# A fourth sum on TensorE in a rational feed-forward behind sketched attention

## The chip, the cores and the metric

The kernel runs on one core of a Trainium2 chip. The metric is the time of one execution on the device in microseconds (us); lower is better. Engines: PE is TensorE (matmuls; PEld its weight loads), DVE is VectorE, ACT is ScalarE, POOL is GpSimd, SP is SyncE, which issues most DMAs. L12 is line 12 of the kernel.

## The reference

Inputs are q, k, v of shape (4 batches, 4 heads, 1088 tokens, 32) in fp32, two sketches S1, S2 of 8 x 32, and the weights of a feed-forward layer: w_in 128 x 2048, w_out 2048 x 128, a (4 numbers) and b (2 numbers). Cut to what matters:

```python
phi(x) = outer(S1 @ x, S2 @ x)                 # 64 features per token and head
kv, z  = sum over tokens of phi(k) * v, phi(k)
x      = (phi(q) @ kv) / (phi(q) @ z + 1e-6)   # heads side by side: 4352 x 128
h      = x @ w_in
g      = (a0 + a1*h + a2*h**2 + a3*h**3) / (1 + |b0|*|h| + |b1|*h**2 + 1e-6)
out    = g @ w_out
```

## The kernel before

**Attention.** For each batch the keys are transposed on DVE in 32 x 32 blocks (`kt`, L255), sketched by TensorE (`ks`, L263), copied by ACT (`kc`, L270), multiplied into features on DVE (`kf`, L275) and summed with v by TensorE (`kp`, L304); ACT keeps the result (`kk`). The queries go in blocks of 256 to 384 tokens, 13 in all: transposition (`qt`, L327), sketches (`qs`), copies (`qc`), features (`qf`), product with kv on TensorE (`qp`, L368), denominator (`qd`, L377 or L380), its inverse (`qi`, L384), quotient on DVE (`qx`, L389), back transposition on TensorE (`qb`, L395), and ACT keeps xT (`qk`, L402). From the fourth block on the sketches take a way through DRAM to be spread over the partitions (L419 to L436).

**Feed-forward.** h and g are kept with the 2048 hidden columns on the partitions, 128 at a time, and tokens along the free axis. The work is cut into 17 units of 4096 elements per partition: unit 0 holds 256 tokens with all 16 column blocks, units 1 to 14 hold 512 tokens with 8 blocks each (two units per group of tokens; the even ones take blocks 8 to 15), units 15 and 16 again 256 tokens with 16 blocks. A unit has two half units of 2048; half unit n belongs to unit n // 2. Steps of a unit, with the letters of the order:

- `h` (L459): TensorE computes a quarter of h in fp32 into one of two PSUM buffers of 1024; `e` (L465): ACT copies it to hh in bf16.
- `u`, `w`, `y` (L488, L494, L499): DVE computes |h|, then |b1||h| + |b0|, then times |h|, for the denominator.
- `ln`, `ex` (L550, L554): ACT computes r = exp(-ln(denominator)), a half unit at a time.
- `p`: the linear factor a3·h + a2, on ACT (`pa`, L545) or DVE (`pd`, L540), as the list P_ON_ACT says.
- `s` (L558): s = h·r. `m` (L562): g = h·s. `x` (L573): g = g·p, thus h·h·r·(a3·h + a2). All on DVE.
- `G` (L592): TensorE adds r with w_out·a0, s with w_out·a1 and g with w_out, three sums per half unit, into one PSUM bank per group of tokens.
- In the half units of HORNER, g = h·p, plus a1 (`v`, L568), times s; only r and g are summed.
- `st` (L601, L609): DVE transposes the bank and four or more DMAs store it.

The scaled copies of w_out are made once, by halves (`wo`, L625 to L629).

**The order.** Nothing is scheduled by the machine: each engine works through its instructions in the order of the list ORDER, which is written out, with the step's name and its unit, block or batch. An engine that waits holds up all that stands behind it. r, s and g have four buffers of a half unit each, p has two, hh three of a unit. Loads are steps too (`lk`, `lq`, `lv`, `lw`, `lx` for k, q, v, w_out and w_in); all of them go into SyncE's queue.

Of the kernel before, what the change touches and what calls it, by code (L numbers as in the profile page):

```python
# [20 lines left out]
ORDER = """
tn:4 tn:0 lw:1 lq:0 kt0:0 lw:0 kt1:0 lx:1 kt2:0 lx:0 ks1:0 kt3:0 ks0:0 lk:1 qt:0 ks2:0 kc0:0 kc1:0 kf0:0 kf1:0 qs:0
kc2:0 qt:1 kf2:0 qc:0 kp0:0 ba:0 kp1:0 qf:0 kp2:0 wo:3 qs:1 kk:0 lv:1 qt:2 qp:0 qc:1 wo:1 qf:1 qs:2 qd:0 qi:0 qc:2
qp:1 qx:0 qf:2 wo:0 qb:0 qp:2 qd:1 qi:1 qk:0 qx:1 qt:3 h3:0 qd:2 qi:2 lq:1 qx:2 wo:4 wo:2 h2:0 e3:0 kt1:1 h0:0 kt0:1
e2:0 pa1:0 u1:0 lk:2 qs:3 w1:0 qb:2 h1:0 y1:0 qc:3 qk:2 e0:0 qt:5 qb:1 ks0:1 qt:4 e1:0 qs:4 qk:1 u0:0 ln1:0 h1:1 qt:6
w0:0 y0:0 kc0:1 ex1:0 h2:1 kf0:1 ks1:1 e1:1 s1:0 e2:1 h0:1 m1:0 kc1:1 ln0:0 kf1:1 h3:1 lq:2 e0:1 x1:0 e3:1 h1:2 kt0:2
ex0:0 u1:1 h2:2 qf:3 w1:1 qc:4 e1:2 qp:3 e2:2 s0:0 pa0:0 h3:2 y1:1 h0:2 qd:3 wo:5 e3:2 qi:3 m0:0 G0:0 e0:2 qx:3 G1:0
ln0:1 kt1:2 x0:0 qb:3 ks0:2 u1:2 qk:3 G2:0 ex0:1 lk:3 pd0:1 G3:0 w1:2 G4:0 pa1:1 kp1:1 y1:2 kc0:2 ln1:1 G5:0 qf:4 lv:2
qs:5 kf0:2 kk:1 ex1:1 qp:4 s0:1 ks1:2 qd:4 qc:5 qi:4 ln0:2 qt:7 G0:1 qx:4 m0:1 qb:4 G1:1 qk:4 s1:1 ex0:2 h3:3 x0:1
kc1:2 h2:3 m1:1 e3:3 kf1:2 h0:3 e2:3 kt1:3 ln1:2 s0:2 h1:3 st:0 m0:2 e0:3 qs:7 x1:1 e1:3 h2:4 ex1:2 u1:3 h3:4 pd1:2  # L30
pa0:2 w1:3 kp1:2 s1:2 e2:4 x0:2 e3:4 h0:4 lv:3 qf:5 pa0:3 y1:3 qp:5 qc:7 e0:4 h1:4 m1:2 qd:5 ln0:3 qi:5 qt:9 G2:1 qx:5
e1:4 x1:2 qb:5 G3:1 qk:5 u1:4 ex0:3 G4:1 m0:3 G5:1 pa1:3 G0:2 w1:4 h0:5 kt0:3 ln1:3 m1:3 h2:5 y1:4 kk:2 ex1:3 ks0:3
G1:2 e0:5 s1:3 G2:2 ln0:4 G3:2 h1:5 v0:3 ex0:4 qf:7 x0:3 G4:2 e2:5 qs:6 s0:4 qc:6 h3:5 e1:5 pd0:4 ln1:4 m0:4 h1:6 v1:3
e3:5 x0:4 pa1:4 h0:6 u1:5 qt:8 G5:2 e1:6 w1:5 ex1:4 h3:6 st:2 y1:5 e0:6 qp:7 e3:6 s1:4 G0:3 pa0:5 lq:3 G2:3 x1:3 qs:8
m1:4 h2:6 ln0:5 m0:5 G3:3 e2:6 x1:4 G5:3 ex0:5 qf:6 G0:4 u1:6 G1:4 qc:8 qd:7 ln1:5 qi:7 qp:6 w1:6 G2:4 qx:7 qd:6 pa0:6
qi:6 v0:5 qb:7 G3:4 qx:6 y1:6 qb:6 qk:7 G4:4 qk:6 ex1:5 h3:7 m0:6 pa1:5 G5:4 s1:5 h1:7 e3:7 st:4 h2:7 m1:5 e1:7 ln0:6
x0:5 h0:7 qt:10 x1:5 e2:7 G0:5 e0:7 qf:8 ks1:3 kc0:3 ex0:6 u1:7 qs:9 h1:8 v0:6 qc:9 w1:7 ln1:6 h3:8 s0:6 e1:8 pd1:6
qp:8 ex1:6 y1:7 h0:8 e3:8 s1:6 kc1:3 ln0:7 h2:8 x0:6 e0:8 m1:6 G2:5 qd:8 ex0:7 G3:5 qi:8 kf0:3 G4:5 kf1:3 G5:5 e2:8
qs:10 ln1:7 u1:8 kp1:3 qx:8 w1:8 ex1:7 qb:8 G0:6 qf:9 qk:8 y1:8 qc:10 h3:9 pa0:7 s0:7 h0:9 e3:9 s1:7 ln0:8 h2:9 qt:12
m0:7 e0:9 G0:7 x1:6 e2:9 h1:10 ex0:8 x0:7 qt:11 h1:9 u1:9 pa0:8 m1:7 G2:6 pd1:7 e1:9 G3:6 s0:8 e1:10 G4:6 u0:9 ln1:8  # L40
h3:10 w1:9 m0:8 qp:9 ex1:8 x1:7 h2:10 x0:8 qd:9 kk:3 e3:10 qi:9 w0:9 pa0:9 h0:10 qf:10 y0:9 qp:10 e2:10 y1:9 e0:10
G5:6 qx:9 qd:10 ln0:9 qi:10 qb:9 s1:8 G1:7 qx:10 G2:7 qk:9 u1:10 ex0:9 G3:7 m1:8 qb:10 G4:7 qk:10 s0:9 ln1:9 G5:7
qs:11 pd1:8 h1:11 w1:10 qc:11 ex1:9 x1:8 h0:11 e1:11 m0:9 pa1:9 h3:11 y1:10 e0:11 G0:8 s1:9 e3:11 h2:11 ln0:10 x0:9
h0:12 m1:9 e2:11 pd0:10 ex0:10 h1:12 u1:11 x1:9 e0:12 G1:8 w1:11 e1:12 G2:8 ln1:10 G3:8 s0:10 G4:8 y1:11 G5:8 ex1:10
qs:12 G0:9 m0:10 G1:9 ln0:11 h3:12 s1:10 ex0:11 x0:10 h2:12 qf:11 pa1:10 m1:10 G2:9 s0:11 G3:9 e3:12 G4:9 x1:10 qc:12
ln1:11 qp:11 pd0:11 m0:11 G5:9 qd:11 e2:12 G0:10 qi:11 x0:11 ex1:11 G1:10 u1:12 G2:10 pa1:11 qx:11 G3:10 w1:12 qb:11
G4:10 qk:11 s1:11 pa0:12 h1:13 y1:12 h3:13 e1:13 m1:11 ln0:12 h2:13 st:6 x1:11 ex0:12 G5:10 qf:12 G0:11 st:8 e3:13
qp:12 s0:12 e2:13 st:10 h0:13 ln1:12 m0:12 u1:13 h2:14 e0:13 x0:12 ex1:12 u0:13 h3:14 w1:13 w0:13 e2:14 y1:13 e3:14
h1:14 pa1:12 y0:13 h0:14 s1:12 qd:12 e1:14 qi:12 m1:12 G1:11 e0:14 qx:12 G2:11 ln1:13 u1:14 qb:12 G3:11 pd0:13 G4:11
ex1:13 w1:14 G5:11 x1:12 G0:12 qk:12 ln0:13 h0:15 s1:13 pd1:13 ex0:13 G1:12 y1:14 G2:12 e0:15 h2:15 s0:13 ln0:14 m1:13  # L50
h3:15 e2:15 m0:13 ex0:14 h1:15 x1:13 x0:13 e3:15 G3:12 s0:14 e1:15 h2:16 ln1:14 u1:15 G4:12 m0:14 ex1:14 G5:12 w1:15
G0:13 h3:16 pa0:14 st:12 y1:15 G1:13 e2:16 G2:13 s1:14 e3:16 h1:16 ln0:15 u2:16 u3:16 w2:16 w3:16 h0:16 x0:14 ex0:15
y2:16 G3:13 pd0:15 e0:16 G4:13 s0:15 e1:16 G5:13 y3:16 pa1:14 G0:15 u0:16 m0:15 G1:15 ln1:15 G0:14 m1:14 G1:14 w0:16
G2:14 ex1:15 x0:15 G3:14 y0:16 G2:15 v1:14 G3:15 ln0:16 s1:15 x1:14 ex0:16 pd1:15 G5:14 m1:15 G0:16 ln2:16 s0:16 G4:15
pa0:16 x1:15 G1:16 ex2:16 m0:16 G5:15 ln3:16 s2:16 x0:16 ex3:16 m2:16 G2:16 pa2:16 st:15 s3:16 G3:16 pa3:16 G4:16
st:14 x2:16 m3:16 G5:16 G6:16 x3:16 G7:16 G8:16 st:16
""".split()
# [12 lines left out]
def kernel(  # L70
    ctx: ExitStack,
# [466 lines left out]
    def d_p(i, h, hh):
        if not on_act(i, first(h)):
            nc.vector.tensor_scalar(out=part_of(i, "p", h), in0=hh, scalar1=a3, scalar2=a2, op0=AX.mult, op1=AX.add)  # L540

    @skip(WIDE_P, on_act)
    def a_p(i, h, hh):
        if on_act(i, first(h)):
            nc.scalar.activation(out=part_of(i, "p", h), in_=hh, func=ACT.Identity, scale=a3_reg, bias=a2)  # L545

# [21 lines left out]
            nc.vector.tensor_scalar(out=g, in0=g, scalar1=a1, scalar2=None, op0=AX.add)  # L568

    @skip(WIDE_X, horner)  # L570
    def d_g(i, h, hh):
        g = part_of(i, "g", h)
        nc.vector.tensor_mul(out=g, in0=g, in1=part_of(i, "s" if horner(i, first(h)) else "p", h))  # L573
# [9 lines left out]

    def gather(i, part):
        t0, tl, f0, per = units[i]
        if t0 not in outs:
            outs[t0] = bank()
            summed[t0] = [0, sum(len(z) for j in range(NU) if units[j][0] == t0 for z in terms(j))]
        for x, y, key in terms(i)[part]:
            done = summed[t0]  # L590
# [1 line left out]
            nc.tensor.matmul(outs[t0][:, :tl], lhsT=w_sb[y][:, f0 + x, :], rhs=part_of(i, key, h)[:, c:c + tl],  # L592
                             start=done[0] == 0, stop=done[0] == done[1] - 1)
# [25 lines left out]
    QC = Queries(0, q0, cuts[2], cuts[3])  # L619

    def w_part(x):
        y, f = x // 2, x % 2 * (nf // 2)
        o, t = w_sb[y][:, f:f + nf // 2], w_out_sb_f[:, f:f + nf // 2]
        if y == 2:
            (nc.scalar.copy if W_ENG[x] else nc.vector.tensor_copy)(out=o, in_=t)  # L625
        elif W_ENG[x]:
            nc.scalar.activation(out=o, in_=t, func=ACT.Copy, scale=a_sb[:, y:y + 1])
        else:
            nc.vector.tensor_scalar(out=o, in0=t, scalar1=a_sb[:, y:y + 1], scalar2=None, op0=AX.mult)  # L629
# [93 lines left out]
```

## Time and profile before

| | |
|---|---|
| median of 3 runs | 270.98 us (270.41 to 271.04) |
| the profiled execution's own time | 271.85 us |
| its span, from the first to the last instruction | 270.1 us |
| busy: PE, DVE, ACT | 252.6, 255.7, 246.9 us |
| granted TensorE clock, mean | 0.99 |

How to read it: the profile shows one execution. A group row gives engine, operation, out<-in, partitions x elements and type, count, then busy us and mean ns of one, then the idle time ahead of it with what ended it. A timeline row gives start, duration, engine, line. Matmul ends are modelled, since matmuls are pipelined. A row of the table of stretches gives for each stretch the busy time of PE, PEld, DVE, ACT and POOL, the granted clock, and the share and GB/s of the DMA.

### The profile page before, as it was taken

How to read it: one execution, taken by the hardware profiler on the slowest of the kernel's cores; microseconds unless marked ns; L12 is line 12 of the kernel's file. 1: busy time of each engine (PE TensorE's matmuls, PEld its weight loads, DVE VectorE, ACT ScalarE, POOL GpSimd, SP SyncE). 2: the span in 40 equal slices, each digit the busy share in tenths (PEclk: the TensorE clock that was granted, in tenths of full speed). 3: DMA queues.
4: the chain of work that ended last, by engine and by line, in shares of the span. 5: the costliest groups of instructions: out<-in, count | busy, mean ns of one | idle time of the engine just before them, and what ended most of it. 6: DMA issues, size and time to landing. Idle time of an engine off the chain costs nothing.

```text
span 270.1 us, 4166 instructions
## 1 busy us (share of the span) xinstructions
PE 252.6 (94%) x1598; PEld 136.0 (50%) x1613; DVE 255.7 (95%) x278; ACT 246.9 (91%) x224; POOL 2.9 (1%) x24
## 2 busy tenths in 40 slices
...
DMA packets 30531, 19.57 MB, mean 72 GB/s; under 512 B 20400, under 2 KB 26672, under 8 KB 30512
## 3 DMA queue, kind: packets, MB, share of 16 engines
q1 hardware_dynamic: 28864, 18.92, 26.8%
...
## 4 chain that ended last, share of the span: by engine, by line
DVE 43%; PE 28%; ACT 12%; issue 8%; DMA 6%; SPq 1%; DVEq 0%; ACTq 0%
PE att_ps L592 14%; PE h_ps L459 12%; DVE w L499 7%; DVE s L558 6%; DVE g L562 6%; DVE g L573 5%; DVE w L494 4%; ACT ln L550 4%; DMA k_sb<-in_k_dram 4%; DVE u L488 4%; ACT hh L465 3%; DVE k_p L275 3%; ACT r L554 3%; DMA q_sb<-in_q_dram 2%; DVE q_pT L436 2%
## 5 line engine op out<-in xcount | busy, mean ns | idle before, releaser
L459 PE MATMUL h_ps<-xT,w_in_sb 128*128 128x512 f32 (+1 forms) x320 | 126.2, 538 | 3.7 <-ACT hh L465 2.8
L459 PEld LDWEIGHTS h_ps<-xT,w_in_sb 128*128 128x128 f32 x320 | 58.2, 190 | 56.7 <-issue 36.9
L465 ACT CAST hh<-h_ps 128x1024 bf16<-128x1024 f32 x68 | 67.7, 1026 | 4.5 <-PE h_ps L459 4.3
L592 PEld LDWEIGHTS <-w_out 128*128 128x128 bf16 x460 | 45.0, 99 | 47.2 <-issue 15.0
L550 ACT ACTIVATE ln<-w 128x2048 f32<-128x2048 bf16 (+1 forms) x35 | 66.1, 1888 | 0.8 <-DVE w L499 0.6
L554 ACT ACTIVATE r<-ln 128x2048 bf16<-128x2048 f32 (+1 forms) x35 | 65.8, 1879 | 0.6
L545 ACT ACTIVATE p<-hh,a_sb 128x2048 bf16<-128x2048 bf16 (+1 forms) x23 | 44.6, 1942 | 0.2 <-DVE g L573 0.2
L558 DVE TENSOR_TENSOR s<-hh,r 128x2048 bf16<-128x2048 bf16 (+2 forms) x33 | 40.9, 1242 | 0.0
L499 DVE TENSOR_TENSOR w<-w,u 128x4096 bf16<-128x4096 bf16 (+2 forms) x22 | 39.3, 1794 | 0.1
L592 PE MATMUL att_ps<-g,w_out 128*128 128x512 bf16 (+1 forms) x155 | 34.8, 350 | 4.6 <-DVE g L573 3.9
L592 PE MATMUL att_ps<-r,w_out 128*128 128x512 bf16 (+1 forms) x155 | 35.1, 354 | 1.1 <-ACT sk_sb L419 0.7
L562 DVE TENSOR_TENSOR g<-hh,s 128x2048 bf16<-128x2048 bf16 (+1 forms) x30 | 35.1, 1172 | 0.0
L573 DVE TENSOR_TENSOR g<-g,p 128x2048 bf16<-128x2048 bf16 (+1 forms) x30 | 35.0, 1173 | 0.1
L592 PE MATMUL att_ps<-s,w_out 128*128 128x512 bf16 (+1 forms) x135 | 29.2, 342 | 0.2
L494 DVE TENSOR_SCALAR w<-u,b_abs 128x4096 bf16<-128x4096 bf16 (+2 forms) x22 | 23.8, 1089 | 0.0
L488 DVE TENSOR_SCALAR u<-hh 128x4096 uint16<-128x4096 uint16 (+2 forms) x22 | 21.2, 968 | 0.0
L368 PEld LDWEIGHTS att_ps<-kvz,q_pT 128*64 128x64 f32 x288 | 9.6, 137 | 7.3 <-DVE q_pT L436 2.0
L368 PE MATMUL att_ps<-kvz,q_pT 128*64 128x66 f32 x288 | 11.5, 226 | 0.1
L255 DVE STREAM_TRANSPOSE kT<-k_sb 128x224 f32<-128x224 f32 (+4 forms) x10 | 5.9, 614 | 4.6 <-DMA k_sb<-in_k_dram 4.6
L304 PEld LDWEIGHTS att_ps<-v_sb,k_p 128*64 128x64 f32 (+1 forms) x288 | 8.8, 138 | 2.4 <-DVE qT L327 1.1
L304 PE MATMUL att_ps<-v_sb,k_p 128*64 128x64 f32 (+1 forms) x288 | 9.3, 223 | 0.7 <-DMA v_sb<-in_v_dram 0.7
L540 DVE TENSOR_SCALAR p<-hh,a_sb 128x2048 bf16<-128x2048 bf16 x12 | 9.7, 804 | 0.0
...
## 6 DMA issues: line engine op xcount, KB each, us to landing
...
```

The source lines that it names most:

```text
L459: nc.tensor.matmul(t[:, x * tl:(x + 1) * tl], lhsT=w_in_sb[:, f * 128:(f + 1) * 128], rhs=xT[:, x_at(t0):x_at(t0) + tl], start=True, stop= ...
L465: nc.scalar.copy(out=live[i]["hh"][:, part * PW:(part + 1) * PW], in_=live[i]["h", part])
L488: nc.vector.tensor_scalar(out=t[:, c].bitcast(U16), in0=live[i]["hh"][:, c].bitcast(U16), scalar1=0x7FFF, scalar2=None, op0=AX.bitwise_and)
L494: nc.vector.tensor_scalar(out=t[:, c], in0=live[i]["u"][:, c], scalar1=ab1, scalar2=ab0, op0=AX.mult, op1=AX.add)
L499: nc.vector.tensor_mul(out=t[:, c], in0=t[:, c], in1=live[i]["u"][:, c])
L545: nc.scalar.activation(out=part_of(i, "p", h), in_=hh, func=ACT.Identity, scale=a3_reg, bias=a2)
L550: nc.scalar.activation(out=t, in_=live[i]["w"][:, span(h)], func=ACT.Ln, bias=1.0 + 1e-6)
L554: nc.scalar.activation(out=part_of(i, "r", h), in_=live[i]["ln"], func=ACT.Exp, scale=-1.0)
L558: nc.vector.tensor_mul(out=part_of(i, "s", h), in0=hh, in1=part_of(i, "r", h))
L562: nc.vector.tensor_mul(out=part_of(i, "g", h), in0=hh, in1=part_of(i, "p" if horner(i, first(h)) else "s", h))
L573: nc.vector.tensor_mul(out=g, in0=g, in1=part_of(i, "s" if horner(i, first(h)) else "p", h))
L592: nc.tensor.matmul(outs[t0][:, :tl], lhsT=w_sb[y][:, f0 + x, :], rhs=part_of(i, key, h)[:, c:c + tl], start=done[0] == 0, stop=done[0] == ...
```

## The change

In 11 of the 34 half units (FOUR) the linear factor p is not formed. There `x` writes h·g = h·h·h·r into a p buffer, `G`'s third part sums g = h·h·r with w_out·a2, and a new step `F` sums h·h·h·r with w_out·a3. Two more scaled copies of w_out are made for this, for column blocks 8 to 15 alone, since all 11 half units lie there. HORNER shrinks from five half units to three (7 and 29 leave it; 29 is in FOUR). P_ON_ACT changes: p is left on DVE in half units 1, 2, 8, 15 and 27. The lists of wide steps M, X and P are emptied; a wide step is formed only where both halves of the unit agree. ORDER is new from end to end. The diff, with ORDER cut to its first lines:

```diff
-tn:4 tn:0 lw:1 lq:0 kt0:0 lw:0 kt1:0 lx:1 kt2:0 lx:0 ks1:0 kt3:0 ks0:0 lk:1 qt:0 ks2:0 kc0:0 kc1:0 kf0:0 kf1:0 qs:0
-kc2:0 qt:1 kf2:0 qc:0 kp0:0 ba:0 kp1:0 qf:0 kp2:0 wo:3 qs:1 kk:0 lv:1 qt:2 qp:0 qc:1 wo:1 qf:1 qs:2 qd:0 qi:0 qc:2
-qp:1 qx:0 qf:2 wo:0 qb:0 qp:2 qd:1 qi:1 qk:0 qx:1 qt:3 h3:0 qd:2 qi:2 lq:1 qx:2 wo:4 wo:2 h2:0 e3:0 kt1:1 h0:0 kt0:1
...
+tn:4 ba:0 kt3:0 tn:0 kt1:0 ks1:0 lq:0 kt0:0 kt2:0 ks0:0 ks2:0 kc1:0 kf1:0 qt:0 kc0:0 lk:1 kf0:0 qs:0 kc2:0 kp0:0 qc:0
+kp1:0 kf2:0 kp2:0 qt:1 qt:2 qs:1 qf:0 kk:0 lx:1 qp:0 kt0:1 qc:1 qd:0 lw:1 qi:0 qx:0 kt1:1 qf:1 qs:2 lw:0 qb:0 qt:3
+ks0:1 qk:0 kc0:1 h3:0 kf0:1 wo:7 wo:3 lx:0 qc:2 h2:0 qs:3 qf:2 wo:4 wo:6 e3:0 lk:2 qp:2 e2:0 wo:2 lq:1 pd1:0 qd:2 wo:1
+u1:0 qp:1 ks1:1 qd:1 qc:3 qi:2 qi:1 kc1:1 qx:2 h0:0 wo:5 qx:1 qb:1 qb:2 e0:0 h1:0 qk:1 w1:0 qk:2 kf1:1 y1:0 e1:0 ln1:0
...
-W_ENG = (1, 1, 0, 0, 0, 1)
-P_ON_ACT = (1, 1, 0, 1, 1, 0, 1, 1, 0, 1, 1, 1, 1, 0, 1, 0, 1, 0, 1, 1, 0, 1, 0, 1, 1, 1, 0, 0, 1, 1, 0, 0, 1, 1)
+W_ENG = (1, 1, 0, 0, 0, 1, 1, 0)
+P_ON_ACT = (1, 0, 0, 1, 1, 0, 1, 1, 0, 1, 1, 1, 1, 1, 1, 0, 1, 0, 1, 1, 0, 1, 1, 1, 1, 1, 1, 0, 1, 1, 1, 0, 1, 1)
-WIDE_M = (5,)
-WIDE_X = (5, 14)
-WIDE_P = (2,)
-HORNER = (6, 7, 10, 12, 29)
+WIDE_M = ()
+WIDE_X = ()
+WIDE_P = ()
+HORNER = (6, 10, 12)
+FOUR = (5, 9, 13, 17, 20, 21, 24, 25, 28, 29, 31)
...
+    w_more = [big.tile([128, nf // 2, d_model], BF, name=f"w_more_{i}") for i in range(2)]
...
     def d_g(i, h, hh):
         g = part_of(i, "g", h)
+        if four(i, first(h)):
+            nc.vector.tensor_mul(out=part_of(i, "p", h), in0=hh, in1=g)
+            return
         nc.vector.tensor_mul(out=g, in0=g, in1=part_of(i, "s" if horner(i, first(h)) else "p", h))
...
-        return [[(x, y, key) for x in range(*c)] if y != 1 or not horner(i, n) else []
-                for n, c in enumerate(cuts) for y, key in enumerate(("r", "s", "g"))]
+        return [[(x, y, key) for x in range(*c)] if (y != 1 or not horner(i, n)) and (y != 3 or four(i, n)) else []
+                for n, c in enumerate(cuts) for y, key in enumerate(("r", "s", "g", "p"))]
 
     def gather(i, part):
+        sums(i, part // 3 * 4 + part % 3)
+
+    def gather_four(i, part):
+        sums(i, part * 4 + 3)
...
-            nc.tensor.matmul(outs[t0][:, :tl], lhsT=w_sb[y][:, f0 + x, :], rhs=part_of(i, key, h)[:, c:c + tl],
+            w = w_sb[y][:, f0 + x, :] if y < 2 or not four(i, part // 4) else w_more[y - 2][:, f0 + x - nf // 2, :]
+            nc.tensor.matmul(outs[t0][:, :tl], lhsT=w, rhs=part_of(i, key, h)[:, c:c + tl],
                              start=done[0] == 0, stop=done[0] == done[1] - 1)
```

More of the change, by code (lines that the diff above doesn't have):

```diff
@@ L21 @@
 ORDER = """
-tn:4 tn:0 lw:1 lq:0 kt0:0 lw:0 kt1:0 lx:1 kt2:0 lx:0 ks1:0 kt3:0 ks0:0 lk:1 qt:0 ks2:0 kc0:0 kc1:0 kf0:0 kf1:0 qs:0
-kc2:0 qt:1 kf2:0 qc:0 kp0:0 ba:0 kp1:0 qf:0 kp2:0 wo:3 qs:1 kk:0 lv:1 qt:2 qp:0 qc:1 wo:1 qf:1 qs:2 qd:0 qi:0 qc:2
-qp:1 qx:0 qf:2 wo:0 qb:0 qp:2 qd:1 qi:1 qk:0 qx:1 qt:3 h3:0 qd:2 qi:2 lq:1 qx:2 wo:4 wo:2 h2:0 e3:0 kt1:1 h0:0 kt0:1
-e2:0 pa1:0 u1:0 lk:2 qs:3 w1:0 qb:2 h1:0 y1:0 qc:3 qk:2 e0:0 qt:5 qb:1 ks0:1 qt:4 e1:0 qs:4 qk:1 u0:0 ln1:0 h1:1 qt:6
-w0:0 y0:0 kc0:1 ex1:0 h2:1 kf0:1 ks1:1 e1:1 s1:0 e2:1 h0:1 m1:0 kc1:1 ln0:0 kf1:1 h3:1 lq:2 e0:1 x1:0 e3:1 h1:2 kt0:2
@@ L27 @@
[L27 to L56, printed above, removed]
+tn:4 ba:0 kt3:0 tn:0 kt1:0 ks1:0 lq:0 kt0:0 kt2:0 ks0:0 ks2:0 kc1:0 kf1:0 qt:0 kc0:0 lk:1 kf0:0 qs:0 kc2:0 kp0:0 qc:0
@@ new lines @@
+kp1:0 kf2:0 kp2:0 qt:1 qt:2 qs:1 qf:0 kk:0 lx:1 qp:0 kt0:1 qc:1 qd:0 lw:1 qi:0 qx:0 kt1:1 qf:1 qs:2 lw:0 qb:0 qt:3
+ks0:1 qk:0 kc0:1 h3:0 kf0:1 wo:7 wo:3 lx:0 qc:2 h2:0 qs:3 qf:2 wo:4 wo:6 e3:0 lk:2 qp:2 e2:0 wo:2 lq:1 pd1:0 qd:2 wo:1
+u1:0 qp:1 ks1:1 qd:1 qc:3 qi:2 qi:1 kc1:1 qx:2 h0:0 wo:5 qx:1 qb:1 qb:2 e0:0 h1:0 qk:1 w1:0 qk:2 kf1:1 y1:0 e1:0 ln1:0
+qt:4 h2:1 qt:5 e2:1 kt0:2 h1:1 u0:0 qs:4 kt1:2 ks0:2 ex1:0 w0:0 qt:6 ks1:2 y0:0 s1:0 kc0:2 qf:3 lv:1 e1:1 qc:4 h0:1
+m1:0 qs:5 kf0:2 x1:0 ln0:0 e0:1 h3:1 qp:3 h3:2 e3:1 u1:1 ex0:0 e3:2 s0:0 h2:2 qd:3 wo:0 pa0:0 qi:3 w1:1 kc1:2 e2:2
@@ new lines @@
+qx:3 kp1:1 y1:1 h1:2 m0:0 kk:1 qf:4 lq:2 qc:5 qb:3 h0:2 ln0:1 qk:3 G4:0 qp:4 G3:0 x0:0 qt:7 e1:2 qd:4 G5:0 qi:4 pd0:1
+qx:4 e0:2 u1:2 qs:7 qt:8 lk:3 qb:4 w1:2 ex0:1 s0:1 kf1:2 G1:0 qk:4 G2:0 h0:3 y1:2 h2:3 pa1:1 kt1:3 ln1:1 G0:0 qf:5
+kt0:3 qc:7 e0:3 e2:3 h1:3 m0:1 h3:3 ex1:1 e1:3 qp:5 s1:1 ln0:2 qd:5 e3:3 ex0:2 h2:4 G0:1 qi:5 m1:1 h3:4 e2:4 qs:6 u1:3
+h1:4 e3:4 G4:1 h0:4 x0:1 qx:5 s0:2 w1:3 qf:7 lv:2 x1:1 qb:5 qc:6 kp1:2 ln1:2 ex1:2 y1:3 e1:4 qt:9 qk:5 e0:4 s1:2 kk:2
+u1:4 st:0 m0:2 h1:5 G2:1 qs:8 ln0:3 qp:7 qf:6 ex0:3 m1:2 G3:1 pa0:2 ks0:3 G1:1 w1:4 qc:8 ln1:3 G0:2 x0:2 qd:7 h3:5
@@ new lines @@
+x1:2 e1:5 y1:4 qp:6 pa0:3 qd:6 e3:5 kc0:3 ex1:3 G3:2 F1:2 h0:5 qi:6 qi:7 h2:5 qx:6 e0:5 e2:5 qx:7 ln0:4 ex0:4 qb:7
+G0:3 m0:3 s1:3 G1:2 pd0:4 pa1:3 G5:1 h0:6 u1:5 kf0:3 m1:3 G4:2 h3:6 w1:5 e0:6 v0:3 lq:3 qk:7 y1:5 ln1:4 G2:2 e3:6 x1:3
+ex1:4 G3:3 s0:4 qb:6 h2:6 qk:6 qf:8 e2:6 G5:2 qs:9 h1:6 G1:4 G0:4 h0:7 m0:4 x0:3 ln0:5 G2:3 qc:9 ex0:5 s1:4 e1:6 ks1:3
+x0:4 m1:4 st:2 lv:3 pa0:5 qp:8 G4:3 u1:6 kc1:3 m0:5 G4:4 x1:4 ln1:5 w1:6 G2:4 h3:7 e0:7 ex1:5 e3:7 qt:11 h1:7 G5:3
+h2:7 qd:8 pa0:6 y1:6 e1:7 qt:10 e2:7 F1:4 h0:8 kf1:3 G5:4 qs:10 s1:5 qi:8 qf:9 ln0:6 pa1:5 qx:8 G3:4 u1:7 m1:5 ex0:6
@@ new lines @@
+h2:8 G4:5 G0:5 qc:10 ln1:6 e0:8 ex1:6 e2:8 kp1:3 m0:6 w1:7 v0:6 G3:5 h3:8 y1:7 st:4 s1:6 qb:8 qp:9 x1:5 kk:3 ln0:7
+m1:6 qk:8 v0:5 h1:8 e3:8 G5:5 x1:6 ex0:7 e1:8 qd:9 pa0:7 G0:6 qf:10 s0:6 h0:9 e0:9 h1:9 ln1:7 u1:8 qi:9 w1:8 x0:6 x0:5
+qp:10 h2:9 G4:6 ex1:7 y1:8 s0:7 F1:6 qd:10 s1:7 e1:9 qs:11 G2:6 u0:9 G5:6 G2:5 qi:10 G3:6 m0:7 h3:9 e2:9 pd1:7 ln0:8
+ex0:8 m1:7 qc:11 h0:10 qx:9 e3:9 ln1:8 s0:8 h3:10 qx:10 qb:9 G3:7 e0:10 e3:10 w0:9 h2:10 qb:10 ex1:8 G0:7 qt:12 y0:9
+G1:7 m0:8 u1:9 s1:8 qk:9 e2:10 x0:7 w1:9 ln0:9 G4:8 qf:11 qs:12 m1:8 qk:10 h1:10 ex0:9 x1:7 e1:10 y1:9 G4:7 h0:11
@@ new lines @@
+qc:12 pa0:8 h2:11 x1:8 ln1:9 qp:11 F1:8 st:6 e0:11 u1:10 G0:8 G5:7 h1:11 qd:11 x0:8 ex1:9 G2:8 s0:9 qi:11 w1:10 e2:11
+h3:11 qx:11 pa1:9 s1:9 e1:11 G1:8 G2:7 y1:10 qb:11 pa0:9 e3:11 qf:12 ln0:10 m0:9 h2:12 G1:9 u1:11 qp:12 h3:12 ex0:10
+m1:9 w1:11 e2:12 ln1:10 G3:8 e3:12 s0:10 x1:9 ex1:10 h0:12 qk:11 G1:10 h1:12 y1:11 x0:9 e0:12 G5:8 G0:9 ln0:11 h3:13
+s1:10 m0:10 e1:12 G4:9 m1:10 x0:10 u1:12 G0:10 G3:9 x1:10 F0:10 G5:9 qd:12 ex0:11 ln1:11 e3:13 ex1:11 h2:13 pa0:11
+G2:10 G3:11 w1:12 s0:11 y1:12 F1:10 qi:12 s1:11 st:8 e2:13 u1:13 qx:12 m1:11 w1:13 h0:13 ln0:12 e0:13 ex0:12 G2:9
@@ new lines @@
+pa1:11 m0:11 h1:13 qb:12 e1:13 h0:14 ln1:12 s0:12 x0:11 G5:10 G3:10 e0:14 h3:14 e3:14 G1:11 m0:12 u0:13 y1:13 x1:11
+h1:14 G4:11 w0:13 x0:12 ex1:12 e1:14 y0:13 qk:12 G4:10 s1:12 ln1:13 h2:14 e2:14 h1:15 st:10 m1:12 u1:14 ex1:13 x1:12
+w1:14 e1:15 s1:13 h0:15 G0:11 h3:15 G5:11 F1:12 ln0:13 y1:14 m1:13 e0:15 e3:15 ex0:13 pd1:13 G3:12 G0:12 h2:15 G1:12
+ln0:14 G2:11 e2:15 ex0:14 s0:13 F0:12 x1:13 pa0:13 u1:15 ln1:14 ex1:14 h1:16 m0:13 w1:15 G4:12 G2:12 G4:13 e1:16 s0:14
+y1:15 h0:16 G0:13 G5:12 m0:14 x0:13 e0:16 h3:16 G2:14 ln0:15 s1:14 G3:13 x0:14 u0:16 G3:14 m1:14 ex0:15 h2:16 w0:16
```

19 lines of the change are left out of this document (14 added, 5 removed).

## The prediction

> **What bounds the kernel now.** I read the busy shares first, then six stretches of the span, the waits of VectorE, and the timeline at both ends.
>
> ```profile
> span 270.1 us, 4166 instructions
> PE 252.6 (94%) x1598; PEld 136.0 (50%) x1613; DVE 255.7 (95%) x278; ACT 246.9 (91%) x224; POOL 2.9 (1%) x24
> ```
> ```profile
> 0.00:17.50 17.50, 14.76 (x195) 9.39 (x195) 10.78 (x27) 6.79 (x17) 2.94 (x24) 1.00 0.80 241
> 17.50:26.80 9.30, 8.77 (x56) 7.11 (x56) 6.45 (x12) 6.47 (x9) 0.00 (x0) 1.00 0.80 203
> 26.80:140.00 113.20, 109.02 (x779) 55.77 (x786) 112.72 (x112) 111.49 (x104) 0.00 (x0) 1.00 0.30 82
> 140.00:250.00 110.00, 107.71 (x484) 54.84 (x491) 109.83 (x111) 109.28 (x88) 0.00 (x0) 1.00 0.15 33
> 250.00:266.80 16.80, 12.34 (x87) 8.90 (x86) 15.94 (x20) 12.89 (x10) 0.00 (x0) 0.90 0.13 19
> 266.80:270.10 3.30, 0.00 (x0) 0.00 (x0) 0.00 (x0) 0.00 (x0) 0.00 (x0) 0.72 0.43 65
> ```
> Columns of the second fence: stretch, length, busy PE, weight loads, DVE, ACT, POOL, granted clock, DMA. Between 26.8 and 250 DVE works 222.55 of 223.2 us: it never waits. ACT idles 2.4 us there. So every microsecond taken from DVE counts at once, as long as ACT (2.4 us of room) and TensorE can follow. Of DVE's 14.4 idle us, 9.6 lie before 26.8, one wait among them:
>
> ```profile
> DVE kT L255 <- DMA k_sb<-in_k_dram: 2.7, 1, 2.7
> ```
> ```profile
> 22.20 1.37 DVE L255 STREAM_TRANSPOSE kT<-k_sb 128x224 f32<-128x224 f32 x2 [2.68 <-DMA k_sb<-in_k_dram]
> 26.77 1.95 ACT L550 ACTIVATE ln<-w 128x2048 f32<-128x2048 bf16 x1
> ```
> ```profile
> 11.41 10.77 DMA k_sb<-in_k_dram
> ```
> The second batch's keys, issued at 11.41, land at 22.2 while DVE stands still (the third fence is from the chain of waits); the first logarithm starts at 26.77.
>
> How much room has TensorE? Its 94% says hardly any. Its rows overlap, though, so I go by the distance from one start to the next:
>
> ```profile
> 245.35 1.04 PE L592 MATMUL att_ps<-r,w_out 128*128 128x256 bf16 x8
> 246.22 1.04 PE L592 MATMUL att_ps<-s,w_out 128*128 128x256 bf16 x8
> 247.10 1.03 PE L592 MATMUL att_ps<-r,w_out 128*128 128x512 bf16 x4
> ```
> ```profile
> 235.85 1.89 PE L459 MATMUL h_ps<-xT,w_in_sb 128*128 128x256 f32 x8
> 237.58 1.03 PE L592 MATMUL att_ps<-s,w_out 128*128 128x512 bf16 x4
> ```
> A w_out sum of one half unit lasts 1.04 but takes 0.87 us (246.22 to 247.10 and the one before). A hidden block of eight 256 wide matmuls lasts 1.89 and takes 1.73. The Trainium skill, "Perfetto Trace Analysis", Identifying the Most-Contended Engine, has the same reservation: matmul busy time is a bad measure of headroom because matmuls are pipelined, while for VectorE and ScalarE occupancy is fair. By busy time the sum would be 252.6 + 11.2 added (below) + 5.0 at the two ends = 268.8 without any idle left, so next to no gain could be had; by starts there is room, as follows.
>
> ```profile
> L459 PE MATMUL h_ps<-xT,w_in_sb 128*128 128x512 f32 x224 | 103.9, 604 | 3.0 <-ACT hh L465 2.6 <-ACT xT L402 0.2
> L459 PE MATMUL h_ps<-xT,w_in_sb 128*128 128x256 f32 x96 | 22.4, 383 | 0.7 <-DMA w_in_sb<-in_moe_w_in_dram 0.5 <-ACT hh L465 0.2
> L368 PE MATMUL att_ps<-kvz,q_pT 128*64 128x66 f32 x240 | 9.2, 226 | 0.1
> ```
> ```profile
> 17.58 5.42 PE L459 MATMUL h_ps<-xT,w_in_sb 128*128 128x256 f32 x24 [0.48 <-DMA w_in_sb<-in_moe_w_in_dram]
> ```
> ```profile
> 266.28 0.45 DVE L601 STREAM_TRANSPOSE out_sb<-att_ps 128x256 f32<-128x256 f32 x1 [0.69 <-PE att_ps L592]
> ```
> From the first hidden matmul (17.58) to the last sum (266.3) are 248.7 us. The work in it: 224 records at 0.43 and 96 at 0.216 are 117; the 316 sums of 512 at 0.217 and 144 of 256 at 0.109 (counted in the instruction order, since records are missing) are 84; the attention matmuls, taken at some nine tenths of their rows' 33 busy us (the L368 row is the largest of them), are an estimated 29.5. That makes 230, and leaves 18.5 us free, not the 6 or so that busy time shows. After the last sum come 3.8 us: transposition and store.
>
> **The change, part by part.** The instruction orders of both kernels give the counts.
>
> ```profile
> L545 ACT ACTIVATE p<-hh,a_sb 128x2048 bf16<-128x2048 bf16 x21 | 42.4, 2019 | 0.2 <-DVE g L573 0.2
> L540 DVE TENSOR_SCALAR p<-hh,a_sb 128x2048 bf16<-128x2048 bf16 x12 | 9.7, 804 | 0.0
> L568 DVE TENSOR_SCALAR g<-g,a_sb 128x2048 bf16<-128x2048 bf16 x5 | 3.7, 732 | 0.0
> L573 DVE TENSOR_TENSOR g<-g,p 128x2048 bf16<-128x2048 bf16 x28 | 33.6, 1209 | 0.0
> L627 ACT ACTIVATE w_out<-w_out_sb_f,a_sb 128x1024 bf16<-128x1024 f32 x2 | 2.3, 1157 | 0.0
> L629 DVE TENSOR_SCALAR w_out<-w_out_sb_f,a_sb 128x1024 bf16<-128x1024 f32 x2 | 1.5, 750 | 0.6 <-DMA w_out_sb_f<-in_moe_w_out_dram 0.6
> ```
> ```profile
> 48.12 0.73 DVE p L540
> 65.69 1.14 DVE g L573
> 94.29 0.66 DVE g L568
> ```
> The second fence is from the chain of waits, where an instruction counts until the next starts: successive DVE instructions overlap by about 0.07 us, and I take 0.07 off each.
> - *Linear factor p.* In 11 half units it is gone. With the new division between engines 5 remain on DVE (12 before) and 18 half units' worth on ACT (22 before). DVE: 7 x 0.73 = -5.1. ACT: 4 x 1.95 = -7.8.
> - *Horner* in 3 instead of 5: the added a1 goes twice, 2 x 0.66 = -1.3 on DVE. Their products stay the same in number.
> - *The product h·h·h·r* takes the place of g·p: same form as L573, 1.21 each, no difference.
> - *Two more scaled halves of w_out*: +0.7 on DVE, +1.1 on ACT.
> - *TensorE:* 11 further sums at 0.87 = 9.5, and the two half units that are no longer Horner sum s as well: 2 x 0.87 = 1.7. Together +11.2.
> - *The wide lists* emptied: costs nothing. By their conditions only the two wide s were ever formed, and these stay.
>
> So DVE -5.7, ACT -6.7, TensorE +11.2.
>
> ```profile
> 10.00:20.00 10.00, 9.34 (x149) 7.74 (x150) 7.92 (x18) 4.82 (x14) 0.00 (x0) 1.00 1.07 327
> ```
> ```profile
> 14.87 0.15 DVE L377 TENSOR_SCALAR den<-att_ps 128x8 f32<-128x8 f32 x1
> 21.31 1.01 ACT L465 CAST hh<-h_ps 128x1024 bf16<-128x1024 f32 x1 [0.71 <-PE h_ps L459]
> ```
> ```profile
> 30.40 1.14 DVE k_p L275
> 33.93 1.40 DVE k_p L275
> ```
> *The start.* SyncE now issues the rest of q, then the second batch's keys, half of w_in, both halves of w_out, the other half of w_in; before, w_out and w_in stood ahead of the keys. DVE has the key transposes (L255) between the first block's q products and its denominator, so that a late landing holds back the first x and the first hidden matmul. Landing: the stretch from 10 to 20 us moved 327 GB/s; ahead are 0.30 MB of q and 0.56 MB of k, 2.6 us from 10, and w_in's half in the kernel before landed some 1.9 us after the same sum: I estimate 14.5 us, against bounds of 12.6 (no lag) and 22.2 (as now). The denominator, at 14.87 now, would come at about 15.5, the first hidden matmul at 17.3: unchanged within 0.5. In return the keys' products (1.14 and 1.40), a w_out half (0.68) and a p (0.74) stand ahead of the first logarithm, and 1.6 us of transposes and absolute values behind it: 2.4 us of DVE work fill what was the wait. Next late is the second hidden evacuation (ending at 22.3 now, about 22.0 then); from it DVE has 5.7 us up to the first logarithm: 27.8 instead of 26.8. Start: -2.4 + 1.0 = -1.4 by DVE.
>
> *New waits.* A p buffer that holds h·h·h·r is released by TensorE's sum and no longer by DVE; behind it waits the next unit's p on ACT, and behind that the logarithms. In the order each such sum stands ahead of that p, and it costs nothing while TensorE is less than a unit (223 us over 17 units, some 13 us) behind; if the cover is gone, an ACT row of 1.95 us is late each time, at most 11 times. I take 0 to 4 us of this into the range.
>
> **The sum.** DVE's bound: 270.1 - 5.7 - 1.4 = 263.0, if it goes on without waits. TensorE's: first hidden matmul 17.3, work 230 + 11.2 + 0.6 (moved behind it at the start) = 242, then 3.8: 263.1, if it never waits. ACT, with 6.7 taken off and 2.4 idle between 26.8 and 250 already, ends no later. So three engines end together, none with room for the others, where before DVE was alone at the limit. Some waiting must come back: bounds 0 and 18.5 (all of today's). I take 4, since TensorE today restarts with a loss of about 0.1 us after each wait (25 waits on hh), and since the tail's last products must be waited for anyway. Span 263 + 4 = 267, that is -3.1. The profiled execution took 271.85 with a span of 270.1, the median of the runs is 270.98; so 270.98 - 3.1 = 267.9, say **268.0**.
>
> The tail today shows what a pause of TensorE costs:
>
> ```profile
> 254.51 0.51 PE L592 MATMUL att_ps<-g,w_out 128*128 128x512 bf16 x1 [2.05 <-DVE g L573]
> ```
> ```profile
> 256.00:258.00 2.00, 2.00 (x10) 1.32 (x9) 2.00 (x3) 2.00 (x2) 0.00 (x0) 0.50 0.00 0
> ```
> After 2.05 us without work the clock is granted at half for a while; a sum then takes twice 0.87. Today it is hidden behind DVE. "TensorE: Matmul & The Clock Gate", The HAM clock gate, in the Trainium skill puts the threshold at one idle window of about 3.4 us; here a pause of 2.05 within busy surroundings was enough, so the measurement decides. It speaks neither for nor against the sum: with a fuller TensorE such pauses grow rarer, and one of them costs some 1.7 us.
>
> **Rivals.**
> 1. *TensorE becomes the bound and keeps its waits* (slower). Its queue is in order: behind a hidden block that waits for one of two h buffers stand the sums, and with seven of the eleven four-fold half units in units 10 to 15 there is no free time there to catch up in. For it: 18.5 us of waiting today, and the hidden matmuls with their weight loads stood 25 times for hh:
>
> ```profile
>   ACT hh L465: 15.8, 25
> ```
> Against it: today's waits are largely those of an engine that is early. Price: 263.1 plus the waits left. From 7 us on nothing is gained; at 10, span 273, time 274.
> 2. *The keys land late* (no change). If they need 4 us more, at 18.5, the first hidden matmul moves from 17.3 to about 21, and with it TensorE's whole chain: 267 + 3.7 = 270.7, time 271.5, of which the fuller start may take some back. For it: 10.77 us from issue to landing today. Against it: 1.6 MB stood ahead then, 0.3 now.
> 3. *The three engines mesh as DVE does now*: waits of 1, span 264, time 265.
> That the change doesn't do what it says is no rival: the orders show the eleven sums and the missing p.
>
> **How the numbers follow.** Forecast (gain of 1 to 5 us) 0.52, rival 3 or better 0.18, rival 2 0.11, rival 1 0.19. Faster by over 0.3% (0.8 us, about what a measurement of this kernel can tell from no change): 0.52 + 0.18 = 0.70; within: rival 2, 0.11; slower: 0.19. The range leaves out the best half of rival 3 and the worse half of rival 1: 264 to 274.
>
> **What would show it.** DVE busy near 250, ACT near 240, TensorE's rows near 264. The key transposes should start at 13 to 16, the first hidden matmul at 17 to 18, the first logarithm at 27 to 29. Between 30 and 250 DVE should show a few us of waits for TensorE or ACT, of which there are none today. Wrong would be: a first hidden matmul after 19 (rival 2); over 7 us of waiting of DVE, with TensorE without a gap (rival 1); TensorE's distance from start to start growing with w_more, which nothing here suggests.

## The result and the profile after

| | before | changed |
|---|---|---|
| median of 20 runs | 271.11 us (270.40 to 272.19) | 270.25 us (268.27 to 271.88) |
| ratio of the times | 1 | 0.9959, 95% interval 0.9939 to 0.9979 |
| profiled execution: time, span | 271.85, 270.1 us | 268.82, 267.0 us |

Faster, by 0.4% (0.3% by the medians) instead of the 1.1% forecast. The spans of the two profiled executions differ by the 3.1 us of the forecast; the medians differ by 0.9. The changed kernel scatters over 3.6 us, the one before over 1.8, and the forecast has no term for that. The changed kernel's executions fall into two groups by their mean granted clock, 11 of 20 at 0.996 or more with a median of 269.1, and 9 at 0.994 or less with a median of 270.9, and the profile is of the first.

The page of the changed kernel, its span and busy shares:

```profile
span 267.0 us, 4248 instructions
PE 257.0 (96%) x1652; PEld 141.6 (53%) x1669; DVE 249.6 (93%) x270; ACT 240.7 (90%) x221; POOL 2.9 (1%) x24
```
The same stretches as before the change (length, busy PE, weight loads, DVE, ACT, POOL, clock, DMA):

```profile
0.00:17.50 17.50, 14.11 (x181) 8.97 (x182) 9.77 (x23) 4.47 (x14) 2.94 (x24) 1.00 0.86 248
17.50:26.80 9.30, 9.30 (x93) 8.08 (x92) 9.29 (x17) 7.61 (x13) 0.00 (x0) 1.00 0.37 135
26.80:140.00 113.20, 112.43 (x813) 58.51 (x821) 109.03 (x110) 110.57 (x106) 0.00 (x0) 1.00 0.40 94
140.00:250.00 110.00, 108.70 (x471) 55.73 (x477) 109.06 (x107) 108.05 (x82) 0.00 (x0) 1.00 0.12 25
```
DVE has lost 6.1 us of work and now idles 5.1 us between 26.8 and 250 (0.65 before); TensorE's rows leave 2.1 us free there (6.5 before). TensorE took over as the bound. Only the first row has grown worse: TensorE works 14.11 us of the first 17.5 (14.76 before), and ACT 4.47 (6.79). The timeline of the changed kernel, from 7 us on, shows why:

```profile
7.21 0.80 PE L265 MATMUL h_ps<-S,kT 128*64 128x64 f32 x20
8.02 0.20 ACT L703 ACTIVATE b_abs<-b_sb 128x2 f32<-128x2 f32 x1 [3.17 <-DMA b_sb<-in_moe_b_dram]
8.59 0.33 ACT L272 COPY b_sk<-att_ps 128x64 f32<-128x64 f32 x2 [0.37 <-issue]
8.83 0.69 DVE L277 TENSOR_TENSOR k_p<-att_ps,b_sk 128x512 f32<-128x512 f32 x1 [1.67 <-ACT b_sk L272]
9.44 0.43 DVE L329 STREAM_TRANSPOSE qT<-q_sb 128x256 f32<-128x256 f32 x1
10.02 1.13 PE L342 MATMUL h_ps<-qT,SAB 64*128 64x256 f32 x8 [2.01 <-DVE qT L329]
13.02 1.06 DVE L257 STREAM_TRANSPOSE kT<-k_sb 128x864 f32<-128x864 f32 x1
17.10 3.72 PE L461 MATMUL h_ps<-xT,w_in_sb 128*128 128x256 f32 x16
```
And the kernel before at the same place:

```profile
6.99 0.33 ACT L270 COPY b_sk<-att_ps 128x64 f32<-128x64 f32 x2 [2.14 <-PE att_ps L263]
8.12 1.25 DVE L275 TENSOR_TENSOR k_p<-att_ps,b_sk 128x512 f32<-128x512 f32 x2
8.34 1.13 PE L340 MATMUL h_ps<-qT,SAB 64*128 64x256 f32 x8 [0.26 <-DVE qT L327]
```
The new order puts the step `ba:0` (absolute value of b, on ACT) second in the list. b's load, the last of five on ACT's queue, lands at 8.0; until then ACT stands, with the copies of the key sketches behind it, DVE with the key products behind those, the transposition of q behind them, and TensorE's query sketches last. The copies come 1.6 us later than before, and TensorE pauses for 2.01 us (0.26 before).

### The profile page after: what moved, and what is told of

Read it like the earlier page. It is cut to its first block, busy times and chain, and to the rows that moved or that the text cites. A ratio compares the mean times of both kernels' runs of the same rounds, so it can differ in the third digit from the quotient of the medians.

```text
span 267.0 us, 4248 instructions
## 1 busy us (share of the span) xinstructions
PE 257.0 (96%) x1652; PEld 141.6 (53%) x1669; DVE 249.6 (93%) x270; ACT 240.7 (90%) x221; POOL 2.9 (1%) x24
## 4 chain that ended last, share of the span: by engine, by line
PE 49%; ACT 19%; DVE 17%; issue 5%; DMA 5%; ACTq 1%; SPq 1%; DVEq 0%
PE h_ps L461 23%; PE att_ps L609 20%; ACT hh L467 6%; ACT r L561 5%; ACT ln L557 4%; DVE g L569 4%; ACT p L552 4%; DVE s L565 2%; DVE g L583 2%; DVE u L490 2%; PE att_ps L370 2%; DMA b_sb<-in_moe_b_dram 2%; DMA b_all<-sk_d 2%; DVE p L581 2%; PE att_ps L306 2%
## 5 line engine op out<-in xcount | busy, mean ns | idle before, releaser
L609 PEld LDWEIGHTS <-w_out 128*128 128x128 bf16 x420 | 40.4, 98 | 42.2 <-issue 14.5
L569 DVE TENSOR_TENSOR g<-hh,s 128x2048 bf16<-128x2048 bf16 (+1 forms) x32 | 37.6, 1180 | 0.2 <-PE att_ps L609 0.2
L552 ACT ACTIVATE p<-hh,a_sb 128x2048 bf16<-128x2048 bf16 (+1 forms) x19 | 36.3, 1919 | 0.0
L583 DVE TENSOR_TENSOR g<-g,p 128x2048 bf16<-128x2048 bf16 (+1 forms) x21 | 24.4, 1168 | 0.0
L609 PE MATMUL att_ps<-g,w_out 128*128 128x512 bf16 (+1 forms) x111 | 23.3, 340 | 0.1
L609 PEld LDWEIGHTS <-w_more 128*128 128x128 bf16 x96 | 9.3, 98 | 11.7 <-issue 3.8
L581 DVE TENSOR_TENSOR p<-hh,g 128x2048 bf16<-128x2048 bf16 x11 | 13.4, 1220 | 0.0
L609 PE MATMUL att_ps<-p,w_more 128*128 128x512 bf16 (+1 forms) x46 | 11.2, 361 | 0.3 <-DVE p L581 0.2
L277 DVE TENSOR_TENSOR k_p<-att_ps,b_sk 128x1024 f32<-128x1024 f32 (+2 forms) x8 | 9.4, 1179 | 1.9 <-ACT b_sk L272 1.9
L609 PE MATMUL att_ps<-g,w_more 128*128 128x512 bf16 (+1 forms) x47 | 11.1, 361 | 0.1
```

The source lines that it names most:

```text
L569: nc.vector.tensor_mul(out=part_of(i, "g", h), in0=hh, in1=part_of(i, "p" if horner(i, first(h)) else "s", h))
L609: nc.tensor.matmul(outs[t0][:, :tl], lhsT=w, rhs=part_of(i, key, h)[:, c:c + tl], start=done[0] == 0, stop=done[0] == done[1] - 1)
```

## The experiments

**Theory A**: that pause is what splits the executions. In some, the half clock is granted behind it, for one window of 3.4 us, and since TensorE is now the bound, the 1.7 us are paid in full. **Theory B**: the landings of the loads at the start scatter, and with them the times.

**e1, the changed kernel again.** 

> The changed kernel unaltered, to see its spread. Over the 20 runs known, 11 with a mean granted clock of 0.996 or more had a median of 269.1 us, 9 with 0.994 or less 270.9. Theory A (one window of half TensorE clock, 3.4 us long and so 1.7 us dear, falls into the working part of some executions): again two groups, 1.6 to 2.0 us apart, each run's clock telling its group; if the profiled execution is of the slow group, a stretch of half clock shows ahead of 260 us. Theory B (DMA landings scatter at the start): times spread evenly over 268 to 272 whatever the clock.

Median 270.91 (268.25 to 272.25) of 12: three at a clock of 0.997 or more took 268.25 to 268.95, nine at 0.990 to 0.994 took 270.47 to 272.25, and nothing lies in between. With nine of 12 at the lower clock the change gains nothing here: the ratio to the kernel before (270.88 on this chip) is 0.9992 (0.9968 to 1.0017).

The groups are as theory A has them, but not all the times are. The medians of the two groups are 2.8 us apart where 1.6 to 2.0 were expected, and in the first sample three executions at 0.997 or more took 270.0 to 271.0. Theory B fits a part of the scatter at full clock: b's absolute value starts at 7.86 us in this run's trace, at 8.02 in the first and at 8.47 in e9's, and the spans of these three, at full clock up to the last sum, are 266.7, 267.0 and 267.5. What makes up the rest stays open.

The kernel before, on the same chip, ran three times at 1.000 (270.63 to 270.84) and 14 times at 0.990 to 0.993 (median 270.97): there the loss of clock, which its profile shows in the tail behind DVE, costs some 0.3 us (0.1 on the chip of the later runs).

**e9 and e10, the changed kernel twice more, for a trace of the other group.** 

> The changed kernel unaltered, one more profile, since all profiles of it so far are of its fast group. Theory A: if its time is above 270, the trace shows half clock for 3.4 us or more beginning at 8 to 14 us and full clock from there to the last sums; below 269.5, full clock throughout. If a slow execution shows full clock up to 250, theory A falls.

 

> The same kernel and the same expectation once more, for the other group of its executions if the first look does not show it.

269.27 and 270.77 us, spans 267.5 and 269.0: one of each. Stretches of e9 (the column after POOL is the granted clock), then of e10:

```profile
6.00:10.00 4.00, 1.58 (x36) 1.29 (x36) 2.20 (x6) 0.53 (x3) 0.00 (x0) 1.00 0.97 235
10.00:14.00 4.00, 3.52 (x82) 3.15 (x84) 4.00 (x7) 1.03 (x4) 0.00 (x0) 1.00 0.96 269
```
```profile
6.00:10.00 4.00, 1.58 (x36) 1.29 (x36) 2.25 (x6) 0.53 (x3) 0.00 (x0) 1.00 0.95 239
10.00:14.00 4.00, 3.57 (x46) 2.94 (x47) 4.00 (x7) 0.88 (x2) 0.00 (x0) 0.61 0.93 259
26.80:140.00 113.20, 113.18 (x814) 59.45 (x813) 109.01 (x109) 110.02 (x107) 0.00 (x0) 1.00 0.39 95
```
From 6 to 10 us the two are alike to 0.05 us (before that, e10's idle matmuls at the start are busy for 4.39 us, e9's for 4.63). Then e10's clock falls to 0.61 on average over 10 to 14 (half, from 10.9 to 14.3), and what follows is alike again. Timeline rows of e9, then of e10:

```profile
10.48 1.13 PE L342 MATMUL h_ps<-qT,SAB 64*128 64x256 f32 x8 [1.84 <-DVE qT L329]
11.54 2.32 PE L306 MATMUL att_ps<-v_sb,k_p 128*64 128x64 f32 x72
13.79 1.14 PE L342 MATMUL h_ps<-qT,SAB 64*128 64x256 f32 x8
...
17.56 3.72 PE L461 MATMUL h_ps<-xT,w_in_sb 128*128 128x256 f32 x16
```
```profile
10.43 1.66 PE L342 MATMUL h_ps<-qT,SAB 64*128 64x256 f32 x8 [1.77 <-DVE qT L329]
12.02 3.34 PE L306 MATMUL att_ps<-v_sb,k_p 128*64 128x64 f32 x72
15.29 1.14 PE L342 MATMUL h_ps<-qT,SAB 64*128 64x256 f32 x8
...
19.05 3.72 PE L461 MATMUL h_ps<-xT,w_in_sb 128*128 128x256 f32 x16
```
In e10 the sketches take 1.59 us up to the next start instead of 1.06, and the values' sums 3.27 instead of 2.25. The first hidden matmul is 1.49 us later, the span 1.5 us longer. The whole difference between these two executions is made ahead of the first hidden matmul and never won back.

**e2, `ba` back to its old place.**

```diff
-tn:4 ba:0 kt3:0 tn:0 ...
-kp1:0 kf2:0 kp2:0 ...
+tn:4 kt3:0 tn:0 ...
+ba:0 kp1:0 kf2:0 kp2:0 ...
```


> The step that takes the absolute value of b on ACT goes back to where it stood before the change, behind the first query copy; else the changed kernel. In the changed profile ACT stands 3.2 us for b's load until 8.02 and the first key products come at 8.83 instead of 8.12, on the chain of waits. If that wait is a term of the missing gain: the first hidden matmul comes 0.6 to 0.9 us earlier than 17.10, and the median falls by about 0.8, to 269.4. Theory A, with TensorE's pause at 8 to 10 us as the trigger: that pause shrinks to about 1.2 us, fewer runs show a clock under 0.995, and the median falls by up to 1.7 more. Theory B, or a trigger elsewhere: as many runs of low clock as in the unaltered kernel.

267.83 us (267.38 to 268.01), ratio to before 0.9878 (0.9861 to 0.9895): more than expected for the wait alone, 2.4 us under the first median of the changed kernel and 3.1 under that of e1. All four clocks are 0.997 or more. Its trace:

```profile
7.19 0.68 DVE L277 TENSOR_TENSOR k_p<-att_ps,b_sk 128x512 f32<-128x512 f32 x1
8.36 1.13 PE L342 MATMUL h_ps<-qT,SAB 64*128 64x256 f32 x8 [0.24 <-DVE qT L329]
16.13 3.72 PE L461 MATMUL h_ps<-xT,w_in_sb 128*128 128x256 f32 x16
```
```profile
26.80:140.00 113.20, 113.17 (x829) 58.70 (x828) 108.96 (x110) 110.57 (x106) 0.00 (x0) 1.00 0.39 94
```
TensorE's pause of 2.01 us has shrunk to 0.24, and the first hidden matmul is at 16.13 instead of 17.10. The span is 0.9 us shorter (266.1): that prices the wait by these two traces. By the executions at full clock on this chip (268.46, the median of three in e1, against 267.83) it is 0.6. TensorE, at 113.17 of 113.20 us, is the bound: what it wins at the start is won at the end.

**e3, the pause filled with idle matmuls, and e4, both edits.**

```diff
-TURNS = (11, 0, 0, 0, 2, 0, 0, 0, 0)
+TURNS = (11, 8, 0, 0, 2, 0, 0, 0, 0)
-... ks2:0 kc1:0 ...
+... ks2:0 tn:1 kc1:0 ...
```


> The changed kernel with 8 idle matmuls of 512 columns (some 1.7 us) on TensorE in its pause from 8.0 to 10.0 us, behind the first batch's key sketches. Theory A with this pause as the trigger: no run with a clock under 0.995, median 269.1 (1.1 less than unaltered), spread under 1.5 us. Trigger elsewhere, or theory B: median 270.2 and the same spread.

 

> Both of these edits together. If both terms are real and add up: median 268.3 to 268.6, all runs at a clock of 0.996 or more. If only the wait for b counts: 269.4. If only the clock counts: 269.1.

e3: 268.81 (268.53 to 269.44, six runs), all clocks at 0.995 or more, 2.1 us under e1. Eight matmuls whose result nobody reads, with the wait for b left in place, take away the group at the lower clock and leave 0.9 us of scatter. The landing of b and the wait for it are untouched, so theory B falls as the cause of the two groups. e4: 268.44, as forecast for both (with one clock of 0.995 where 0.996 or more was expected), but 0.6 above e2: with the wait gone the idle matmuls stand in TensorE's way, ahead of the query sketches. They are a remedy only while the pause is there.

**e5, the pause made longer.** b's load goes to SyncE's queue behind the values' loads.

```diff
-    nc.scalar.dma_start(out=b_sb, ...)
     load_v(0)
+    nc.sync.dma_start(out=b_sb, ...)
```


> The changed kernel with the load of b issued later, on SyncE's queue behind the values' four loads; the absolute value of b stays at its early place on ACT. It lengthens the wait at about 5 to 8 us to about 10, and TensorE's pause to some 4 us. Theory A (the pause is what halves the clock): every execution shows it; the trace has a stretch of 3.4 us at half clock starting at 10 to 13 us, all clocks are at 0.995 or less, and the time is 268 (the version without the wait) + 3 for the wait + 1.7 for the clock, about 272.5, with a small spread. If the pause has nothing to do with it: 271 to 272 on top of the two groups of the unaltered kernel, and full clock at 10 to 14.

273.1 us (272.1 to 273.93, ten runs, clocks 0.984 to 0.991). TensorE waits 3.6 us, and now every execution loses clock; the trace:

```profile
10.00:14.00 4.00, 1.96 (x8) 1.28 (x8) 3.15 (x5) 0.82 (x4) 0.00 (x0) 0.69 0.92 258
14.00:18.00 4.00, 4.00 (x74) 3.92 (x72) 2.28 (x4) 0.58 (x1) 0.00 (x0) 0.50 1.05 321
26.80:250.00 223.20, 220.92 (x1302) 116.23 (x1313) 217.74 (x219) 217.51 (x193) 0.00 (x0) 1.00 0.25 60
```
Half clock lasts two windows here instead of one (11.5 to 18.4), and the time is 0.6 us more than expected. Judged by their mean clocks, a pause of some 2 us halves the clock in 18 of the 32 runs of the first sample and of e1, one of some 3.6 us in all ten.

**e8, the early `ba` in the kernel before.**

```diff
-tn:4 tn:0 lw:1 lq:0 ...  ...  kp0:0 ba:0 kp1:0 ...
+tn:4 ba:0 tn:0 lw:1 lq:0 ...  ...  kp0:0 kp1:0 ...
```


> The kernel before, with the absolute value of b on ACT moved to the front, as in the changed kernel. There DVE waits until 22.2 for the second batch's keys, whatever happens ahead. If that wait covers it: 270.9 to 271.2, no change. If the step costs there what it costs in the changed kernel: 271.7 from the wait alone, up to 273 with the clock.

272.17 us, ratio 1.0046 (1.0027 to 1.0066): the cover does not hold. Its timeline:

```profile
21.09 1.37 DVE L255 STREAM_TRANSPOSE kT<-k_sb 128x224 f32<-128x224 f32 x2 [0.53 <-DMA k_sb<-in_k_dram]
23.14 0.69 DVE L488 TENSOR_SCALAR u<-hh 128x2048 uint16<-128x2048 uint16 x1 [0.68 <-ACT hh L465]
27.55 1.95 ACT L550 ACTIVATE ln<-w 128x2048 f32<-128x2048 bf16 x1
```
The keys are there at 21.09 in this execution (22.20 before) and the wait for them shrinks to 0.53, but next late is the hidden evacuation, and the first logarithm comes 0.8 us later than 26.77. The median is 1.1 us above that of the kernel before (271.07 on this chip): the early `ba` costs something there too. Two of the 12, at clocks of 0.993 and 0.994, took 273.5 and 273.7.

**e7, eight four-fold half units instead of eleven** (5, 9 and 13 form p on DVE again; `ba` as in e2).

```diff
-FOUR = (5, 9, 13, 17, 20, 21, 24, 25, 28, 29, 31)
+FOUR = (17, 20, 21, 24, 25, 28, 29, 31)
```


> As e2 (b's absolute value back), with eight four-fold half units instead of eleven: in 5, 9 and 13 p is formed again, on DVE. TensorE 2.6 us less, DVE 2.2 more. If TensorE is the bound, as its rows without a gap from 26.8 to 250 say: 265.3 to 267, at least 1 us under e2's 267.8. If DVE is still the bound: 269 to 270. If the three are evenly coupled: 267.5 to 268.2.

267.37 us (266.99 to 267.6), ratio to before 0.9861 (0.9831 to 0.9892), the fastest kernel here; 0.46 under e2, so between "TensorE bound" and "evenly coupled". The two ran on different chips, and the intervals of their ratios to the kernel before overlap, so e7's lead over e2 is not shown by the times; its span is 0.9 us shorter (265.2). Its stretches:

```profile
26.80:140.00 113.20, 111.57 (x816) 58.40 (x823) 111.63 (x113) 111.34 (x106) 0.00 (x0) 1.00 0.38 93
140.00:250.00 110.00, 107.76 (x460) 55.44 (x468) 109.06 (x107) 107.46 (x83) 0.00 (x0) 1.00 0.12 25
```
Where three sums were taken out (26.8 to 140), the three engines are within 0.3 us of each other: 2.6 us less on TensorE bought at most some 0.9 us, since DVE and ACT then stand in the way.

**e6, the new order without any four-fold sum** (`ba` as in e2; p put in ahead of the product before its use; in half unit 28 g is summed before p is multiplied in, the product itself is still formed).

> The new order with b's absolute value back at its old place, but no half unit summed four-fold: p is formed again in the 11 half units (5, 13, 17, 20 and 31 on DVE, the other six on ACT, ahead of the product that precedes its use), the 11 extra sums and the two extra copies of w_out are gone. TensorE 9.5 us less, DVE +3.0, ACT +10.6. If the gain comes from the four-fold sums: ACT becomes the bound, 270 to 273. If the order alone gains: 267 or less.

278.27 us, outside all that was expected. ACT works 250.3 us and DVE 252.8 of a span of 276.7; neither is full. Two of DVE's waits show a part of the reason:

```profile
DVE g L583 <- ACT p L552: 4.5, 3, 2.6
DVE g L569 <- ACT p L552: 2.1, 1, 2.1
```
These 6.6 us are waits for p from ACT, into whose queue I put six more by hand; DVE idles 23.9 us in all, and every execution loses clock (0.974 to 0.985). So the run shows only that this order does not serve without the four-fold sums. What an order made without them would take, and so how much of the gain is the sums' and how much the new order's, stays open.

## Why the prediction was right and wrong

**The work and the three bounds: right.** DVE 255.7 to 249.6 (-6.1, forecast -5.7), ACT 246.9 to 240.7 (-6.2, forecast -6.7). TensorE's busy time rose by 4.4 only, though 11.2 us of sums were added by starts: the room was there, as the distance between starts said and busy time did not. By busy time the forecast would have been next to no gain. First hidden matmul 17.10 (17.3), first logarithm:

```profile
27.80 1.91 ACT L557 ACTIVATE ln<-w 128x2048 f32<-128x2048 bf16 x1
```
(27.8 forecast). From 17.10 to the last sum at 262.7 are 245.6 us, 3.6 more than the 242 of work, where 4 of waiting was taken. The trace lists only 1.6 us of TensorE's waits in this stretch, so whether the rest is waiting or work that the estimate lacked is not shown. Span 267.0, as forecast. *New waits*: p on ACT, released by TensorE, shows no idle time ahead of it at all:

```profile
L552 ACT ACTIVATE p<-hh,a_sb 128x2048 bf16<-128x2048 bf16 (+1 forms) x19 | 36.3, 1919 | 0.0
```

**The step that failed: *The start*.** It listed what SyncE's queue is moved past, but not that ACT's queue has a step moved to its front whose operand arrives last; the wait for b and TensorE's pause behind it stand in the sum at nothing. The wait cost 0.6 to 0.9 us of span (e2) and the pause behind it 1.49 us of half clock (e10) in some half of the executions. That the first hidden matmul came at 17.10, with 17.3 forecast, was luck: the keys landed in time for a transposition at 13.02 (14.5 forecast), which alone would have put the first hidden matmul at about 16.1, as e2 shows; the wait for b took 1.0 of it back.

**The sentence that failed with it**: "with a fuller TensorE such pauses grow rarer, and one of them costs some 1.7 us". The price was about right (1.49 in e10), the frequency wrong. I looked for the pause where it stood before, in the tail behind DVE. In the tail of the changed kernel it is gone, but the new wait made one of 2 us at the start, on TensorE's own chain, and in about half of the executions the half clock follows it. Had I followed `ba:0` through ACT's queue, the query sketches' pause would have been in the sum.

**The last conversion failed too.** It took the difference of two spans off the median before, which lay 0.9 us below the profiled execution (270.98 against 271.85). A span of 267.0 takes 268.82 us, not 268.0.

**The rivals.** Rival 2, late keys, did not occur, though its mechanism (a load at the head of an in-order queue, ahead of the first x) is what happened, with another load on another engine. Rival 1 was right in its premise, TensorE is the bound, and wrong in its price: at most 3.6 us of waits of TensorE, 5.1 idle us of DVE, and not over 7. Rival 3 is not reached even by e7.

**The account** of the missing 2.2 us (270.25 against 268.0): 0.8 is the conversion, the distance from 268.0 to the profiled execution's 268.82. The other 1.4 lie between that execution, at full clock up to the last sum, and the median of 20, of which nine lost clock. The wait for b itself is not among the 2.2: it lies within the span of 267.0, where the early keys made up for it. So e2, with that wait undone, is at 267.83 partly by luck: its span is 0.9 us shorter than the one forecast, and the conversion had taken 0.8 too much off.
